# Two layer-1 blocks to a PSUM bank and one relu, quad-wise copies of the folded W_in, and a new early order, in a fused attention and squared-relu MLP

## The chip, the core and the metric

The kernel runs on one core of one Trainium2 chip. Its time is the device time of one execution in microseconds, the median of three runs. A profiled execution is a run of its own, with a time of its own and a span from the first to the last instruction. The engines, each with an instruction stream of its own that it works through in order: TensorE (PE, matmul), VectorE (DVE), ScalarE (ACT), GpSimd (POOL) and SyncE (SP). POOL issues all loads but that of the first p, and SP the stores.

## The reference

For each of 8 batches and 8 heads there are 576 rows of q, k and v (64 wide) and 32 rows of p. A first attention packs k and v into 32 rows; a second one lets q attend to these; the result, 4608 tokens of 512 numbers, goes through a two-layer MLP with a squared relu.

```python
p_packed = softmax(p @ k.T / 8) @ v              # 32 x 64 a head
x        = softmax(q @ p_packed.T / 8) @ p_packed  # 576 x 64 a head
h = x @ w_in            # x: [4608, 512], w_in: [512, 2048]
r = maximum(h, 0)
out = (r * r) @ w_out   # [4608, 512], float32
```

## The kernel before

**Names.** The order of all work is written out by hand: `ORDER` (L48) is a string of words, and `run` (L815) emits the instructions of one word after another, so that each engine gets its own in the order of the words. A word is a step, its numbers, and behind a colon the engine (`v` DVE, `a` ACT, `p` POOL). The heads of a batch are worked in two groups of four, called quads below: `m101` is the step `m1` of batch 0, quad 1.

**First attention of a batch.** `Lk`, `Lv`: loads (L291, L305). `kT`: DVE transposes k (L354). `s1`: scores on PE (L414). `m1`, `x1`: max (DVE, L437) and exponential (ACT, L451). `eT`, `eo`: PE transposes the exponentials, and a copy brings them out of PSUM (L461, L477). `pv`, `rd`, `pp`: times v, reciprocal, scaling (L488, L485, L519). `pt`, `po`: transpose of the packed rows and copy (L538, L546). `bd`, `bs` make a second form of them (L522, L530).

**Folding.** The packed rows are multiplied into W_in: `w`N (L616) makes the quarter N (512 of the 2048 columns) of a batch's own `wp` in two PSUM banks, one for each quad, and `W`N (L626) copies it out, both quads in one instruction of 1024 columns, or, with a third digit, one quad of 512 columns. `W201` is quarter 2 of batch 0, quad 1. W_in itself is loaded in six pieces `Wi` (L257): columns 0 to 511 and 512 to 1023 by 256 KB a quad, the last 1024 by 512 KB a quad. Quarters 2 and 3 need the last two pieces.

**Second attention.** `Lq` or `LA`, `LB`: loads of q (L275). Batches 0 and 1 are cut into a part A of 256 rows and a part B of 320 (`CUTS`, L40). For batch 0, PE transposes q (`QA`, `QB`, L371) and ACT copies it out (`EA`, `EB`); elsewhere DVE does it (`qA`, `qB`, `qT`). `z` or `s2`: scores on PE. `t`, `m`, `s`, `x`, `u`, `a`, `T` with A, B or 2: transpose, max, subtraction, exponential (ACT), sum with reciprocal, scaling, and the transpose that gives `a2T`, the operand of layer 1.

**The MLP.** `h`b.part.n (L650) makes block n (128 of the 2048 hidden columns) of a part: two matmuls (L638), one for each quad, of 256 or 320 columns in the first two batches, into a bank of its own. `r` (L656) is its relu, out of PSUM. `q` (L674) squares two blocks at once, SBUF to SBUF, into `gT`. `o`t.j (L685) is two matmuls of 512 columns for 128 tokens t; eight of them fill a bank, `c` copies it out and `d` stores it. Part A of batch 0 has tokens 0 to 255 (`o0`, `o1`). `H` and `R` (L662, L669) do two blocks with one relu; no word of `ORDER` uses them before.

**PSUM.** Eight banks: `psa` is two tiles of two banks each, for the attention's matmuls and `w`. Of the other four, three ("spare") and one ("idle") serve batch 0's attention and the fillers; from the first layer block on they are `x` and `y`, two banks each. The blocks of batch 0 take an `x` bank when n is even and a `y` bank when it is odd, those of later batches `y`; `o` takes `y` for t below 2 and `x` beyond. A bank is given out again when the last reader of the tile before it is done, and a step that needs one waits for that.

**Fillers.** `Z`n.m (L337) is n matmuls of 512 and m of 256 columns on zeros; nobody uses their result.

```python
    def busy(self, n, short):

        ps = self.banks("idle").tile([P, 512], F32, name="ps_idle")
        for m in [self.NE] * n + [self.NE // 2] * short:
```

The functions around the change:

Of the kernel before, what the change touches and what calls it, by code (L numbers as in the profile page):

```python
# [48 lines left out]
pf Lk00 P0 Lk01 kT00 Z14.0 s100 Lv00 LA0 kT01 m100 Z1.1 s101 m101 I x100 Lv01 x101 P1 Z2.1 eT00 LB0 eo00:v Z0.1 eT01  # L49
QA01 QA00 eo01:v Wi01 EA00:a rd0 pv0 pp0 EA01:a Z1.0 pt0 Wi00 po0:v Z0.1 zA0 tA00 Wi11 tA01 mA00 Z1.0 QB01 QB00 EB00:a  # L50
EB01:a mA01 sA00:v Wi10 Wi20 Z2.1 zB0 sA01:v xA00 xA01 tB00 Z5.0 w00 tB01 Wi21 mB00 W001:a Z3.0 w10 uA01 uA00 mB01
sB00:p aA01:p xB00 W000:a TA01 sB01:v aA00:p TA00 Lk11 uB00 W100:a h0.0.2 h0.0.3 Lk10 h0.0.0 xB01 h0.0.1 W101:a r0.0.3:a
h0.0.5 aB00:p uB01 Wo0 r0.0.2:a r0.0.0:v r0.0.1:a aB01:v h0.0.6 h0.0.7 h0.0.4 r0.0.5:a r0.0.6:a TB00 TB01 r0.0.4:v Lv10
r0.0.7:a h0.1.3 r0.1.3:a h0.1.6 q0.0.3:v h0.1.5 r0.1.6:v q0.0.0:v q0.0.2:v h0.1.2 h0.1.1 q0.0.1:a h0.1.0 r0.1.2:a w20
r0.1.5:a w30 r0.1.0:v h0.1.7 r0.1.1:a W30:a W20:v h0.1.4 Lv11 kT11 r0.1.4:a r0.1.7:a h0.0.9 h0.0.8 r0.0.9:a r0.0.8:a
h0.1.14 r0.1.14:a h0.1.15 q0.1.0:a q0.1.2:v kT10 Wo1 h0.0.13 r0.1.15:v h0.0.14 h0.0.12 q0.0.4:v q0.1.1:p s11 h0.0.11
r0.0.12:a h0.0.10 LB1 r0.0.13:a h0.1.13 r0.0.14:a m111 m110 r0.0.11:a h0.1.8 h0.0.15 r0.0.10:a x111 o2.0 x110 o2.1
r0.0.15:v r0.1.13:v eT11 h0.1.11 q0.0.5:v h0.1.9 q0.1.7:p r0.1.8:v eT10 r0.1.11:a rd1 h0.1.10 o0.0 r0.1.9:v eo11:a o1.0
LA1 eo10:v pv1 r0.1.10:v h0.1.12 pp1 q0.1.3:a o1.1 o0.1 bd1 r0.1.12:a pt1 q0.0.6:v o3.0 o3.1 q0.1.4:v po1:v w31 qB10 w11
q0.0.7:a o3.2 o1.2 qB11 W11:a o0.2 q0.1.6:v o0.3 W31:a qA10 o2.2 zB1 qA11 tB10 zA1 tA11 tB11 o3.3 tA10 Wo2 o2.3 mA10  # L60
mA11 o1.3 w21 mB10 mB11 q0.1.5:a Wo3 w01 sA11:v W21:a sA10:v xA11 sB11:v o2.4 uA11 o1.4 xA10 o1.5 uA10 o0.4 sB10:v o0.5
xB11 o0.6 o0.7 Pr o2.5 o1.6 aA10:v W01:a c0:a xB10 aA11:v Lk20 d0 TA10 TA11 o1.7 o3.4 Lv21 Lv20 uB11 c1:a o2.6 h1.0.1
Lk21 h1.0.6 Px o2.7 r1.0.1:v d1 r1.0.6:v o3.5 aB11:v h1.0.0 c2:a h1.0.2 Pt o3.6 r1.0.0:a TB11 o3.7 r1.0.2:a d2 Lk31 Pu
q1.0.0:a h1.0.4 h1.0.3 c3:a o4.0 r1.0.3:v r1.0.4:a o5.0 kT20 q1.0.1:a h1.0.7 d3 h1.0.5 uB10 o5.1 r1.0.5:a o4.1 r1.0.7:v
q1.0.2:a aB10:v h1.0.10 h1.0.8 q1.0.3:v r1.0.10:a o4.2 kT21 Lq2 h1.0.9 r1.0.8:a o5.2 r1.0.9:a h1.0.12 TB10 s12 q1.0.4:v
r1.0.12:a h1.0.14 m120 o5.3 Lv30 r1.0.14:a h1.1.1 m121 h1.1.3 r1.1.1:a o5.4 x120 r1.1.3:v h1.0.11 o4.3 r1.0.11:v x121
h1.1.7 kT31 h1.0.15 eT20 Lq3 q1.0.5:a o4.4 r1.0.15:v eT21 r1.1.7:v q1.0.7:a o5.5 rd2 eo20:v eo21:a h1.0.13 h1.1.2
r1.0.13:v o4.5 r1.1.2:v q1.0.6:a h1.1.6 pv2 r1.1.6:v h1.1.8 pp2 h1.1.0 q1.1.1:a r1.1.8:v Lk30 o5.6 qT21 q1.1.3:a o4.6
h1.1.12 r1.1.0:a bd2 pt2 qT20 o4.7 bs2:a Lk40 h1.1.5 po2:v r1.1.12:a o5.7 q1.1.0:v c4:a h1.1.10 r1.1.5:v c5:a s22 d4
r1.1.10:v h1.1.4 o6.0 t221 r1.1.4:a h1.1.9 d5 o7.0 q1.1.2:a t220 h1.1.13 r1.1.9:a o6.1 qT30 r1.1.13:a Lq4 h1.1.11  # L70
q1.1.4:a m221 w22 w32 r1.1.11:a o6.2 m220 W32:a h1.1.14 h1.1.15 W22:v Lv31 o6.3 r1.1.14:a q1.1.6:a o7.1 o6.4 sb21:v
r1.1.15:a Lv40 o7.2 q1.1.5:a kT30 o7.3 q1.1.7:a o7.4 sb20:v Lk41 x221 o6.5 qT31 o7.5 x220 o6.6 su21 o6.7 o7.6 su20 c6:a
o7.7 w02 a221:v c7:a d6 w12 o8.0 W02:a a220:v o8.1 d7 o8.2 aT21 W12:a o8.3 aT20 o8.4 Lq5 h2.0.1 h2.0.0 r2.0.1:v o8.5
r2.0.0:a o8.6 q2.0.0:v h2.0.2 h2.0.3 r2.0.2:v o9.0 Lk50 o8.7 r2.0.3:v h2.0.5 c8:a s13 q2.0.1:v r2.0.5:a h2.0.4 d8 m130
o10.0 r2.0.4:a h2.0.6 kT40 h2.0.7 r2.0.6:a o10.1 r2.0.7:a q2.0.2:v h2.0.10 Lk51 x130 m131 o9.1 h2.0.8 r2.0.10:a q2.0.3:v
o9.2 r2.0.8:a kT41 h2.0.13 x131 eT30 h2.0.9 r2.0.13:v o10.2 eo30:a rd3 r2.0.9:v h2.1.1 eT31 q2.0.4:v h2.0.14 r2.1.1:a
o10.3 r2.0.14:v eo31:a h2.0.11 Lk61 o9.3 r2.0.11:v o9.4 h2.0.12 h2.1.5 q2.0.5:v r2.0.12:a pv3 r2.1.5:v h2.0.15 q2.0.6:v
h2.1.4 pp3 r2.0.15:a o9.5 r2.1.4:v h2.1.6 bd3 pt3 q2.0.7:v h2.1.0 bs3:a o9.6 r2.1.6:v r2.1.0:v Lv41 po3:a o9.7 q2.1.2:v
# [56 lines left out]
class Kernel:  # L135
# [526 lines left out]
    def step_hh(self, engine, b, hf, fp):  # L662

        s0, s1 = self.part(b, hf)
        ps = self.ph[b, hf, fp, 2] = self.turn32("ps_hh")[:, :, :s1 - s0]
        for i in range(2):
            self.layer1(ps[:, i], b, 2 * fp + i, s0, s1)
# [202 lines left out]
```

## Time and profile before

| | |
|---|---|
| median of 3 runs | 240.57 us (240.53 to 240.69) |
| the profiled execution | 241.25 us |
| its span, first to last instruction | 239.4 us |
| busy: PE, DVE, ACT, POOL | 230.2, 200.2, 143.8, 72.4 us |
| first layer block of batch 0 (`h0.0.2`) starts | 20.65 us |
| first layer block of batch 1 (`h1.0.1`) starts | 47.56 us |
| loads: queue, share of 16 DMA engines | POOL's, 53.1% |
| moved from 15 to 20 us | 206 GB/s |

In a row of a timeline stand the start in us from the span's beginning, the length in us, the engine, the line of the kernel, the operation, what it writes and reads, the shape, and how many instructions follow each other in that row; behind it in brackets how long the engine was idle before, and what ended that. A wait that is put down to an engine that had long been done was ended by something else, often a DMA. The waits of an engine are listed as total, number and longest. Ends of matmuls are modelled, and a matmul is longer than the time to the next one's start.

### The profile page before, as it was taken

The page shows a single profiled execution, that of the slowest core. Times are in us where ns is not written, and L with a number is a line of the kernel's source. Part 1 is how long each engine was busy: PE and PEld are TensorE (multiplying, and loading weights), DVE is VectorE, ACT ScalarE, POOL GpSimd, SP SyncE. Part 2 cuts the span into 40 slices and gives each one's busy share as a digit, 9 for nine tenths or more (in the row PEclk, how much of TensorE's full clock was granted, in tenths as well). Part 3 has the DMA queues.
Part 4 walks back from the last instruction along what each step waited for, and adds up shares of the span by engine and source line. Part 5 has one row for each costly group of instructions (what it writes and reads, how often), then busy time and mean ns, then how long its engine had stood idle before and what let it go on. Part 6 is the DMA issues. An engine that isn't in the chain of part 4 may idle for free.

```text
span 239.4 us, 5971 instructions
## 1 busy us (share of the span) xinstructions
PE 230.2 (96%) x2355; PEld 123.7 (52%) x2355; DVE 200.2 (84%) x455; ACT 143.8 (60%) x311; POOL 72.4 (30%) x122
## 2 busy tenths in 40 slices
PE   8876999999999999999999999999999999999994
PEld 2533563456544564456555554565545644555543
DVE  2768986998997889989998889997899789987740
ACT  2347974887797657865693648774485346733300
POOL 8509573786676334054303340002000000000000
PEclk9999999999999999999999999999999999999999
DMA  6999999999999978469923993216112212111224
GB/s 103 195 205 214 204 211 204 152 246 190 198 208 183 239 98 120 69 85 202 123 68 36 201 131 55 52 43 96 44 24 67 49 44 45 45 45 45 49 60 111
DMA packets 30331, 28.50 MB, mean 119 GB/s; under 512 B 8160, under 2 KB 24288, under 8 KB 30304
## 3 DMA queue, kind: packets, MB, share of 16 engines
q0 software_dynamic: 23776, 18.55, 53.1%
q1 hardware_dynamic: 6384, 9.51, 14.9%
q8 instruction: 18, 0.29, 0.5%
q10 hardware_dynamic: 144, 0.07, 0.1%
q14 instruction: 9, 0.07, 0.1%
HBM read 37.22 MB, written 9.44 MB: 195 GB/s over the span
## 4 chain that ended last, share of the span: by engine, by line
PE 88%; DMA 5%; POOL 2%; DVE 1%; issue 1%; ACT 1%; ACTq 0%; POOLq 0%
PE ps_o L695 52%; PE ps_h L638 26%; DMA w_in_bf<-in_moe_w_in_dram 5%; PE ps_wp L623 3%; PE ps_s L411 3%; PE ps_e1T L474 2%; PE ps_pv L507 1%; POOL w_in_bf L259 1%; POOL q_b L271 1%; DVE r L645 1%; POOL k_b L271 1%; DVE wp L459 0%; ACT wp L457 0%; PE ps_pv L500 0%; PE ps_o L700 0%
## 5 line engine op out<-in xcount | busy, mean ns | idle before, releaser
L695 PE MATMUL ps_o<-w_out_bf,gT 128*128 128x512 bf16 (+1 forms) x576 | 147.0, 378 | 0.0
L638 PE MATMUL ps_h<-a2T,wp 128*128 128x288 bf16 (+2 forms) x512 | 89.7, 286 | 1.4 <-ACT r L643 0.9
L643 ACT ACTIVATE r<-ps_h 128x288 bf16<-128x288 f32 (+2 forms) x161 | 61.4, 413 | 48.5 <-PE ps_h L638 42.5
L695 PEld LDWEIGHTS <-gT 128*128 128x128 bf16 x576 | 54.5, 98 | 43.8 <-issue 3.3
L638 PEld LDWEIGHTS <-wp 128*128 128x128 bf16 x512 | 47.4, 98 | 42.5 <-issue 8.0
L645 DVE TENSOR_SCALAR r<-ps_h 128x288 bf16<-128x288 f32 (+2 forms) x95 | 41.3, 449 | 11.7 <-PE ps_h L638 10.5
L683 DVE TENSOR_TENSOR gT<-r 128x576 bf16<-128x576 bf16 (+2 forms) x108 | 46.5, 444 | 2.3 <-ACT r L643 1.4
L457 ACT CAST wp<-ps_wp 128x1024 bf16<-128x1024 f32 (+1 forms) x31 | 29.2, 962 | 9.5 <-PE ps_wp L623 9.5
L457 ACT COPY o_sb<-ps_o 128x512 f32<-128x512 f32 x26 | 15.2, 589 | 12.1 <-PE ps_o L695 11.7
L271 POOL DMA_DIRECT2D k_b<-in_k_dram x28 | 15.4, 554 | 14.4 <-DVE kT L357 6.8
L319 POOL DMA_DIRECT2D v_b<-in_v_dram x12 | 9.4, 782 | 34.1 <-PE ps_pv L507 28.5
L271 POOL DMA_DIRECT2D q_b<-in_q_dram x16 | 11.0, 690 | 25.3 <-DVE qT L369 23.4
L451 ACT ACTIVATE e<-ps_s,nm 128x576 bf16<-128x576 f32 x16 | 11.8, 742 | 7.0 <-DVE nm L437 6.8
L357 DVE STREAM_TRANSPOSE kT<-k_b 128x576 uint32<-128x576 uint32 x16 | 12.3, 771 | 3.0 <-DMA k_b<-in_k_dram 3.0
L591 DVE TENSOR_REDUCE sums<-e 128x18 f32<-128x576 f32 (+2 forms) x20 | 12.1, 606 | 0.6 <-ACT e L585 0.6
L681 ACT ACTIVATE gT<-r 128x640 bf16<-128x640 bf16 (+1 forms) x18 | 12.2, 694 | 0.4 <-DVE r L645 0.2
L437 DVE TENSOR_REDUCE nm<-ps_s 128x1 f32<-128x576 f32 x16 | 11.5, 739 | 1.0 <-PE ps_s L411 0.8
L341 PE MATMUL ps_idle<-gT 128*128 128x512 bf16 (+1 forms) x34 | 11.1, 458 | 1.2 <-DVE gT L190 1.2
L585 ACT ACTIVATE e<-d 128x576 f32<-128x576 f32 (+2 forms) x20 | 11.7, 600 | 0.8 <-DVE d L579 0.8
L369 DVE STREAM_TRANSPOSE qT<-q_b 128x576 uint32<-128x576 uint32 (+2 forms) x16 | 10.8, 683 | 1.1 <-DMA q_b<-in_q_dram 1.1
L579 DVE TENSOR_TENSOR d<-s,mx 128x576 f32<-128x576 f32 (+2 forms) x19 | 11.7, 641 | 0.0
L573 DVE TENSOR_REDUCE mx<-s 128x18 f32<-128x576 f32 (+2 forms) x20 | 11.6, 609 | 0.0
(68 smaller groups left out, 174.6 us busy)
## 6 DMA issues: line engine op xcount, KB each, us to landing
out_dram<-o_sb SPq DMA_DIRECT2D x65, 128.0 KB, 2.4
v_b<-in_v_dram POOLq DMA_DIRECT2D x12, 256.0 KB, 5.6
w_out_bf<-in_moe_w_out_dram POOLq DMA_DIRECT2D x4, 512.0 KB, 10.7
q_b<-in_q_dram POOLq DMA_DIRECT2D x6, 288.0 KB, 6.1
q_b<-in_q_dram POOLq DMA_DIRECT2D x12, 144.0 KB, 6.9
k_b<-in_k_dram POOLq DMA_DIRECT2D x12, 108.0 KB, 4.7
gT<-in_v_dram POOLq DMA_DIRECT2D x4, 288.0 KB, 8.5
w_in_bf<-in_moe_w_in_dram POOLq DMA_DIRECT2D x4, 256.0 KB, 11.7
```

What stands on the lines that cost most here:

```text
L271: engine.dma_start(x[n:], s[:P - n])
L357: self.nc.vector.transpose(t["kT"][:].rearrange("p s e -> p (s e)").bitcast(U32), t["k"][:].rearrange("p t d -> p (t d)").bitcast(U32))
L451: self.nc.scalar.activation(out, x, ACT.Exp, bias=t["nm"], accum_out=self.den[b][:, qd:qd + 1])
L457: engine.copy(out, x)
L579: engine.tensor_tensor(out=d2[:, x], in0=t["s2"][:, x], in1=t["mx"][:, x].unsqueeze(2).to_broadcast([P, n, NP]), op=ALU.subtract)
L591: nc.vector.reduce_sum(out=sums[:, x], in_=t["e2"][:, x], axis=AX.X)
L638: self.nc.tensor.matmul(ps, lhsT=self.att[b, 0]["wp"][:, qd, fb * P:(fb + 1) * P], rhs=self.att[b, qd]["a2T"][:, s0:s1], start=(qd == 0), ...
L643: engine.activation(r, ps, ACT.Relu)
L645: engine.tensor_scalar_max(r, ps, 0.0)
L681: engine.activation(out, r, ACT.Square)
L683: engine.tensor_tensor(out=out, in0=r, in1=r, op=ALU.mult)
L695: self.nc.tensor.matmul(self.o[tt][:, e], lhsT=self.gT[:, fb, a:a + P], rhs=self.w_out_bf[:, fb, e], start=(i == 0), stop=(i == self.NFB - 1))
```

## The change

- The sixteen blocks of batch 0's part A are made by eight `H` and taken out by eight `R`, all on ACT. `step_hh` takes one bank of `x` (odd pair) or `y` (even pair) for batch 0, with two blocks of 256 columns side by side, instead of a tile of `psa`. Before, sixteen `h` and sixteen `r`, thirteen of these on ACT and three on DVE.
- Quarters 2 and 3 of batch 0's `wp` are copied by quads, `W201` and `W301` on DVE, `W200` and `W300` on ACT. Before, `W20` on DVE and `W30` on ACT, 1024 columns each.
- The words ahead of `h2.0.1` stand in another order. Some go to another engine: `eo00`, `po1`, `W22` to ACT, `bs2`, `eo21` to DVE, and a number of relus and squares of batches 0 and 1 either way. `Lk11` and `Lk10` stand ahead of `sB00:p` on POOL, `Wi00` ahead of `Wi01`, `Lq2` ahead of `Lk21` and of batch 2's v's, `Lk31` behind `Lv31`; SP's stores go 2, 3, 1, 0, 4, 6, 5, 7. `QB00` stands ahead of `QB01`. `kT31` is the last DVE word ahead of batch 2's first relu.
- Fillers: three of 512 columns fewer and one of 256 more, and `w00` stands ahead of most of them.

From `h2.0.1` on both orders have the same words.

```diff
@@ -46,43 +46,42 @@ (ORDER; behind h2.0.1 the words are the same)
-pf Lk00 P0 Lk01 kT00 Z14.0 s100 Lv00 LA0 kT01 m100 Z1.1 s101 m101 I x100 Lv01 x101 P1 Z2.1 eT00 LB0 eo00:v Z0.1 eT01
-QA01 QA00 eo01:v Wi01 EA00:a rd0 pv0 pp0 EA01:a Z1.0 pt0 Wi00 po0:v Z0.1 zA0 tA00 Wi11 tA01 mA00 Z1.0 QB01 QB00 EB00:a
-EB01:a mA01 sA00:v Wi10 Wi20 Z2.1 zB0 sA01:v xA00 xA01 tB00 Z5.0 w00 tB01 Wi21 mB00 W001:a Z3.0 w10 uA01 uA00 mB01
-sB00:p aA01:p xB00 W000:a TA01 sB01:v aA00:p TA00 Lk11 uB00 W100:a h0.0.2 h0.0.3 Lk10 h0.0.0 xB01 h0.0.1 W101:a r0.0.3:a
-h0.0.5 aB00:p uB01 Wo0 r0.0.2:a r0.0.0:v r0.0.1:a aB01:v h0.0.6 h0.0.7 h0.0.4 r0.0.5:a r0.0.6:a TB00 TB01 r0.0.4:v Lv10
-r0.0.7:a h0.1.3 r0.1.3:a h0.1.6 q0.0.3:v h0.1.5 r0.1.6:v q0.0.0:v q0.0.2:v h0.1.2 h0.1.1 q0.0.1:a h0.1.0 r0.1.2:a w20
-r0.1.5:a w30 r0.1.0:v h0.1.7 r0.1.1:a W30:a W20:v h0.1.4 Lv11 kT11 r0.1.4:a r0.1.7:a h0.0.9 h0.0.8 r0.0.9:a r0.0.8:a
-h0.1.14 r0.1.14:a h0.1.15 q0.1.0:a q0.1.2:v kT10 Wo1 h0.0.13 r0.1.15:v h0.0.14 h0.0.12 q0.0.4:v q0.1.1:p s11 h0.0.11
-r0.0.12:a h0.0.10 LB1 r0.0.13:a h0.1.13 r0.0.14:a m111 m110 r0.0.11:a h0.1.8 h0.0.15 r0.0.10:a x111 o2.0 x110 o2.1
-r0.0.15:v r0.1.13:v eT11 h0.1.11 q0.0.5:v h0.1.9 q0.1.7:p r0.1.8:v eT10 r0.1.11:a rd1 h0.1.10 o0.0 r0.1.9:v eo11:a o1.0
-LA1 eo10:v pv1 r0.1.10:v h0.1.12 pp1 q0.1.3:a o1.1 o0.1 bd1 r0.1.12:a pt1 q0.0.6:v o3.0 o3.1 q0.1.4:v po1:v w31 qB10 w11
-q0.0.7:a o3.2 o1.2 qB11 W11:a o0.2 q0.1.6:v o0.3 W31:a qA10 o2.2 zB1 qA11 tB10 zA1 tA11 tB11 o3.3 tA10 Wo2 o2.3 mA10
-mA11 o1.3 w21 mB10 mB11 q0.1.5:a Wo3 w01 sA11:v W21:a sA10:v xA11 sB11:v o2.4 uA11 o1.4 xA10 o1.5 uA10 o0.4 sB10:v o0.5
-xB11 o0.6 o0.7 Pr o2.5 o1.6 aA10:v W01:a c0:a xB10 aA11:v Lk20 d0 TA10 TA11 o1.7 o3.4 Lv21 Lv20 uB11 c1:a o2.6 h1.0.1
-Lk21 h1.0.6 Px o2.7 r1.0.1:v d1 r1.0.6:v o3.5 aB11:v h1.0.0 c2:a h1.0.2 Pt o3.6 r1.0.0:a TB11 o3.7 r1.0.2:a d2 Lk31 Pu
-q1.0.0:a h1.0.4 h1.0.3 c3:a o4.0 r1.0.3:v r1.0.4:a o5.0 kT20 q1.0.1:a h1.0.7 d3 h1.0.5 uB10 o5.1 r1.0.5:a o4.1 r1.0.7:v
-q1.0.2:a aB10:v h1.0.10 h1.0.8 q1.0.3:v r1.0.10:a o4.2 kT21 Lq2 h1.0.9 r1.0.8:a o5.2 r1.0.9:a h1.0.12 TB10 s12 q1.0.4:v
-r1.0.12:a h1.0.14 m120 o5.3 Lv30 r1.0.14:a h1.1.1 m121 h1.1.3 r1.1.1:a o5.4 x120 r1.1.3:v h1.0.11 o4.3 r1.0.11:v x121
-h1.1.7 kT31 h1.0.15 eT20 Lq3 q1.0.5:a o4.4 r1.0.15:v eT21 r1.1.7:v q1.0.7:a o5.5 rd2 eo20:v eo21:a h1.0.13 h1.1.2
-r1.0.13:v o4.5 r1.1.2:v q1.0.6:a h1.1.6 pv2 r1.1.6:v h1.1.8 pp2 h1.1.0 q1.1.1:a r1.1.8:v Lk30 o5.6 qT21 q1.1.3:a o4.6
-h1.1.12 r1.1.0:a bd2 pt2 qT20 o4.7 bs2:a Lk40 h1.1.5 po2:v r1.1.12:a o5.7 q1.1.0:v c4:a h1.1.10 r1.1.5:v c5:a s22 d4
-r1.1.10:v h1.1.4 o6.0 t221 r1.1.4:a h1.1.9 d5 o7.0 q1.1.2:a t220 h1.1.13 r1.1.9:a o6.1 qT30 r1.1.13:a Lq4 h1.1.11
-q1.1.4:a m221 w22 w32 r1.1.11:a o6.2 m220 W32:a h1.1.14 h1.1.15 W22:v Lv31 o6.3 r1.1.14:a q1.1.6:a o7.1 o6.4 sb21:v
-r1.1.15:a Lv40 o7.2 q1.1.5:a kT30 o7.3 q1.1.7:a o7.4 sb20:v Lk41 x221 o6.5 qT31 o7.5 x220 o6.6 su21 o6.7 o7.6 su20 c6:a
-o7.7 w02 a221:v c7:a d6 w12 o8.0 W02:a a220:v o8.1 d7 o8.2 aT21 W12:a o8.3 aT20 o8.4 Lq5 h2.0.1 h2.0.0 r2.0.1:v o8.5
+pf Lk00 P0 Lk01 kT00 Z14.0 s100 Lv00 LA0 kT01 m100 Z0.1 s101 m101 I x100 Lv01 x101 P1 Z2.1 eT00 Z0.1 eT01 eo00:a QA00
+LB0 Wi00 eo01:v Wi01 QA01 pv0 Wi11 rd0 pp0 Wi10 EA00:a Z1.0 pt0 Wi20 EA01:a Wi21 po0:v Z0.1 zA0 Z1.0 QB00 tA01 tA00
+EB00:a mA01 Lk11 QB01 mA00 EB01:a sA01:v sA00:v xA00 Z1.1 zB0 xA01 tB00 tB01 mB00 w00 mB01 Lk10 uA00 uA01 sB01:v sB00:p
+W000:a aA00:p TA00 xB00 W001:a aA01:p Z7.1 w10 uB00 xB01 W101:a W100:a TA01 H0.0.1 aB00:p H0.0.2 uB01 Wo0 H0.0.0 H0.0.3
+R0.0.1:a R0.0.2:a R0.0.0:a aB01:v TB00 TB01 q0.0.0:v h0.1.1 h0.1.6 q0.0.1:v R0.0.3:a h0.1.5 q0.0.2:v r0.1.6:a h0.1.0
+h0.1.2 r0.1.1:a h0.1.7 r0.1.0:a q0.0.3:v Lv11 r0.1.5:v r0.1.2:a w20 h0.1.3 q0.1.0:v Lv10 w30 W201:v r0.1.7:a W200:a
+h0.1.4 r0.1.3:a W301:v H0.0.4 W300:a kT11 kT10 r0.1.4:a R0.0.4:a H0.0.7 q0.1.2:a h0.1.15 Wo1 h0.1.14 q0.0.4:v H0.0.6
+R0.0.7:a r0.1.15:a s11 H0.0.5 R0.0.6:a q0.1.1:p r0.1.14:v h0.1.11 R0.0.5:a h0.1.13 LB1 o2.0 m111 x111 h0.1.8 q0.1.7:p
+m110 r0.1.13:v x110 LA1 Wo2 o2.1 h0.1.9 r0.1.8:v eT11 h0.1.10 q0.0.6:v eT10 r0.1.9:v r0.1.11:a o1.0 eo11:a r0.1.10:v
+o1.1 h0.1.12 eo10:v q0.1.3:v rd1 pv1 pp1 o0.0 r0.1.12:a bd1 qB11 Wo3 o3.0 pt1 q0.0.7:v o0.1 o2.2 o1.2 po1:a q0.1.6:a
+qB10 qA10 w31 w11 o2.3 qA11 W31:a o3.1 W11:a o3.2 o3.3 zB1 zA1 q0.0.5:a tB11 tA10 tA11 Pr tB10 q0.1.4:a Lk20 o0.2 mA10
+mA11 o0.3 mB10 o1.3 w01 sA10:v w21 o1.4 o0.4 Lq2 sA11:v sB10:v W01:a o0.5 o2.4 o1.5 o1.6 o1.7 xA10 q0.1.5:a o0.6 o0.7
+xA11 uA10 o2.5 Lk21 o3.4 o3.5 aA10:v W21:a uA11 xB10 mB11 sB11:v aA11:v TA10 c1:a Lv21 TA11 c0:a uB10 xB11 h1.0.1 h1.0.0
+o2.6 r1.0.1:a o2.7 h1.0.2 r1.0.0:a uB11 Px h1.0.6 o3.6 o3.7 r1.0.2:v h1.0.3 c2:a r1.0.6:a q1.0.0:v h1.0.4 c3:a aB10:v
+r1.0.3:a r1.0.4:a kT20 o4.0 o5.0 TB10 h1.0.5 r1.0.5:a q1.0.1:v h1.0.12 Pt r1.0.12:v o5.1 o4.1 h1.0.9 Lv20 q1.0.2:a
+h1.0.7 r1.0.9:a o5.2 o4.2 aB11:v h1.0.10 Pu Lk30 TB11 Lq3 r1.0.7:a q1.0.3:a r1.0.10:a h1.0.8 kT21 r1.0.8:a s12 h1.1.1
+q1.0.4:a r1.1.1:a h1.0.14 m120 r1.0.14:v m121 o4.3 x120 o5.3 h1.1.7 r1.1.7:v h1.0.11 o4.4 qT21 eT20 r1.0.11:a h1.1.3
+h1.0.13 x121 Lv30 r1.1.3:v q1.0.5:v eo20:v o5.4 eT21 h1.1.0 eo21:v r1.0.13:a q1.0.6:a r1.1.0:a d2 qT20 h1.0.15 o4.5 d3
+r1.0.15:a o4.6 q1.1.0:a h1.1.12 r1.1.12:a h1.1.8 kT30 pv2 q1.0.7:a rd2 r1.1.8:v d1 h1.1.9 o5.5 pp2 bd2 r1.1.9:a h1.1.5
+o4.7 h1.1.2 r1.1.5:a bs2:v pt2 r1.1.2:a po2:v o5.6 c4:a s22 h1.1.13 q1.1.1:a h1.1.4 o5.7 o7.0 t220 r1.1.4:a q1.1.4:a
+r1.1.13:v h1.1.15 m220 h1.1.11 o7.1 w22 t221 w32 r1.1.15:a r1.1.11:a c5:a qT31 h1.1.10 d0 h1.1.6 o6.0 m221 r1.1.10:a
+q1.1.2:a o6.1 Lk40 r1.1.6:a h1.1.14 sb21:v o6.2 o7.2 q1.1.3:v W22:a o6.3 o7.3 r1.1.14:a o7.4 Lq4 o6.4 q1.1.5:v sb20:v
+Lv31 o7.5 x221 q1.1.6:a q1.1.7:v su21 x220 o6.5 o6.6 a221:v Lk31 o7.6 o6.7 qT30 w12 W32:a w02 su20 a220:v d4 o7.7 c6:a
+aT20 o8.0 d6 W02:a aT21 c7:a Lk41 d5 W12:a d7 o8.1 Lv40 o8.2 o8.3 Lq5 o8.4 kT31 h2.0.1 h2.0.0 r2.0.1:v o8.5 r2.0.0:a
...
@@ -662,7 +661,11 @@
     def step_hh(self, engine, b, hf, fp):
 
         s0, s1 = self.part(b, hf)
-        ps = self.ph[b, hf, fp, 2] = self.turn32("ps_hh")[:, :, :s1 - s0]
+        if b:
+            ps = self.turn32("ps_hh")
+        else:
+            ps = self.bank("x" if fp % 2 else "y", "ps_hh").rearrange("p (i s) -> p i s", i=2)
+        ps = self.ph[b, hf, fp, 2] = ps[:, :, :s1 - s0]
         for i in range(2):
             self.layer1(ps[:, i], b, 2 * fp + i, s0, s1)
 ```

## The prediction

> **What bounds the kernel now.** I read the page's engine table first, then the waits of TensorE (PE), then the timelines of the first 50 us engine by engine.
>
> ```profile
> span 239.4 us, 5971 instructions
> ...
> PE 230.2 (96%) x2355; PEld 123.7 (52%) x2355; DVE 200.2 (84%) x455; ACT 143.8 (60%) x311; POOL 72.4 (30%) x122
> ```
>
> The program is a stream of matmuls with next to no hole in it. All of PE's waits for the other engines' copies and for DMA sit at the start:
>
> ```profile
> PE ps_wp L623 <- DMA w_in_bf<-in_moe_w_in_dram: 1.3, 1, 1.3
> ...
> PE ps_h L638 <- ACT r L643: 0.9, 1, 0.9
> PE ps_h L638 <- DVE wp L459: 0.6, 1, 0.6
> ```
>
> The change removes no real matmul, so it can gain only what PE waits from the first layer block on, and lose only by new waits. The stretch in question, PE's timeline (start, length):
>
> ```profile
> 1.19 5.82 PE L341 MATMUL ps_idle<-gT 128*128 128x512 bf16 x14 [1.19 <-DVE gT L190]
> ...
> 16.43 0.26 PE L397 MATMUL ps_s<-qT,ppT 64*32 64x160 bf16 x8 [0.33 <-ACT qT L457]
> ...
> 17.86 0.41 PE L623 MATMUL ps_wp<-w_in_bf,ppT 64*32 64x512 bf16 x8
> ...
> 20.31 0.41 PE L623 MATMUL ps_wp<-w_in_bf,ppT 64*32 64x512 bf16 x8 [1.29 <-DMA w_in_bf<-in_moe_w_in_dram]
> 20.65 1.05 PE L638 MATMUL ps_h<-a2T,wp 128*128 128x256 bf16 x8
> 22.56 2.83 PE L638 MATMUL ps_h<-a2T,wp 128*128 128x256 bf16 x20 [0.86 <-ACT r L643]
> ...
> 27.17 1.85 PE L638 MATMUL ps_h<-a2T,wp 128*128 128x256 bf16 x14 [0.58 <-DVE wp L459]
> 28.95 0.71 PE L411 MATMUL ps_s<-kT,pT 32*32 32x192 bf16 x48
> ...
> 39.77 0.70 PE L411 MATMUL ps_s<-qT,ppd 32*32 32x320 bf16 x32
> ...
> 42.37 5.35 PE L695 MATMUL ps_o<-w_out_bf,gT 128*128 128x512 bf16 x24
> 47.56 0.60 PE L638 MATMUL ps_h<-a2T,wp 128*128 128x256 bf16 x4
> ```
>
> Prices from it: a 512-column matmul holds PE for (47.56-42.37)/24 = 0.216 us, a step `o` (two) 0.43; a 256-column layer matmul 0.108, so a block 0.22; a 320-column one 0.135, a block 0.27.
>
> **Fixed points.** Four moments in this stretch are set by DMA, which moves 206 to 213 GB/s from 15 us on whatever the order:
>
> ```profile
> 15.00:20.00 5.00, 3.45 (x37) 1.14 (x33) 4.50 (x15) 3.40 (x7) 1.86 (x4) 1.00 1.18 206
> 20.00:25.00 5.00, 3.83 (x35) 2.64 (x36) 4.28 (x14) 4.06 (x12) 4.76 (x9) 1.00 1.13 213
> ```
>
> Four views of loads: one narrowed to W_in's second piece (issue and time to landing, 11.4), one to its last piece (14.1), the DMA issues of 5 to 25 us (the 288 KB of k for kT10, 7.0), and POOL's timeline, which has the issue times of the last two:
>
> ```profile
> L259 POOL DMA_DIRECT2D w_in_bf<-in_moe_w_in_dram x1: 637/637/637, 6.4 to 6.4; - x1
> ...
> DMA to landing us min/median/max: 11.4/11.4/11.4
> ```
> ```profile
> DMA to landing us min/median/max: 14.1/14.1/14.1
> ```
> ```profile
> k_b<-in_k_dram POOLq DMA_DIRECT2D x1, 288.0 KB, 7.0
> ```
> ```profile
> 11.07 0.61 POOL L259 DMA_DIRECT2D w_in_bf<-in_moe_w_in_dram  x1 [0.66 <-DMA q_b<-in_q_dram]
> 18.14 0.72 POOL L579 TENSOR_TENSOR d<-s,mx 128x320 f32<-128x320 f32 x1 [6.45 <-DVE mx L573]
> ...
> 21.02 0.56 POOL L271 DMA_DIRECT2D k_b<-in_k_dram  x1
> ```
>
> So `w00` can't start before 6.4+11.4 = 17.8, `w10` not before 20.3 (its wait says so), `w20` not before 11.07+14.1 = 25.2, and kT10 not before 21.02+7.0 = 28.0. The other two engines of the stretch:
>
> ```profile
> 20.79 0.58 ACT L457 CAST wp<-ps_wp 128x512 bf16<-128x512 f32 x1 [0.96 <-PE ps_wp L623]
> 21.27 0.47 ACT L585 ACTIVATE e<-d 128x320 f32<-128x320 f32 x1
> ...
> 22.11 1.80 ACT L643 ACTIVATE r<-ps_h 128x256 bf16<-128x256 f32 x6
> ...
> 24.91 1.08 ACT L643 ACTIVATE r<-ps_h 128x320 bf16<-128x320 f32 x3
> 26.01 1.01 ACT L457 CAST wp<-ps_wp 128x1024 bf16<-128x1024 f32 x1
> ...
> 33.06 0.79 ACT L457 COPY e1T<-ps_e1T 96x768 bf16<-96x768 bf16 x1
> ```
> ```profile
> 19.47 0.31 DVE L613 STREAM_TRANSPOSE a2T<-a 128x128 uint32<-128x128 uint32 x1
> ...
> 20.28 0.30 DVE L613 STREAM_TRANSPOSE a2T<-a 128x128 uint32<-128x128 uint32 x1
> ...
> 21.78 0.49 DVE L591 TENSOR_REDUCE sums<-e 128x10 f32<-128x320 f32 x1 [0.59 <-ACT e L585]
> ...
> 23.12 0.56 DVE L613 STREAM_TRANSPOSE a2T<-a 128x160 uint32<-128x160 uint32 x2
> ...
> 25.90 1.21 DVE L459 CAST wp<-ps_wp 128x1024 bf16<-128x1024 f32 x1
> ...
> 28.10 0.77 DVE L357 STREAM_TRANSPOSE kT<-k_b 128x576 uint32<-128x576 uint32 x1
> ...
> 38.80 0.77 DVE L369 STREAM_TRANSPOSE qT<-q_b 128x256 uint32<-128x256 uint32 x2
> 40.33 1.58 DVE L568 STREAM_TRANSPOSE s<-ps_s 128x320 f32<-128x320 f32 x4 [0.75 <-PE ps_s L411]
> ...
> 46.57 0.50 DVE L613 STREAM_TRANSPOSE a2T<-a 128x128 uint32<-128x128 uint32 x2
> ```
>
> **The change, step by step.**
>
> *Up to `w10`.* `eo00` goes from DVE to ACT (0.79 by the row at 33.06); ACT is free there and DVE takes only `eo01`, so nothing moves. `EB00` comes after five transposes of ten, and `zB0` waited for it (0.33 at 16.43): an estimate of 0.3 gained, `zB0` ends at 16.4 instead of 16.7, and DVE's `tB00` begins so much earlier. `w00` still starts at 17.9: the fillers around it only change places, and PE now idles 1.5 us where it ran fillers. `Z7.1` (7x0.216+0.11, from 18.2) ends by 20.1, ahead of 20.3. Gain: 0.
>
> *POOL's queue.* The wait at 11.07 shows eight loads in flight: the 12th waits for the 4th. Lk11 and Lk10 now stand ahead of `sB00:p`. Their last issue waits for the 7th load, the first of W_in, which lands one 256 KB piece (1.3 us) ahead of 17.8, at 16.5, and is over by 17.1. `sB00:p` needs the max of `tB00`, near 17.8. Behind the wait stand `sB00`, `aA00`, `aA01`, `aB00` and Wo0; ACT's `xB00` and DVE's `TA` and `TB` wait for them. No cost; were that landing at 17.8, issue and all, `sB00` and its chain would come 0.6 late. DMA is full either way, so the k's land when they did.
>
> *The first blocks.* `TA01` was at 19.47, `TA00` at 20.28. DVE does the same work ahead of `TA00` but `TA01` (0.3), and begins 0.3 earlier: `TA00` at 19.7; then a sum with its reciprocal (0.49 and some 0.2), `TA01` 20.5 to 20.8. `H0.0.1` starts at 20.65 and waits 0.1 for `TA01`. `H0.0.2` needs both quads of `w10`, copied 20.79 and 21.27 (0.58 each): 21.9. So PE waits 0.6 there instead of 1.0 (21.5 to 22.56). Four H's are in four banks and wait for no relu. The other three H's take 1.3, and `h0.1` begins at 23.2 (was 23.5: eight blocks' matmuls of 0.108 from 22.56). Its `TB` were at 23.12, since `uB01` waited 0.59 for `xB01`, then behind W101 on ACT; now `xB01` is ahead of it, and `TB` end near 22.3.
>
> *The relus.* 16 relus of 256 become 8 of 512. Before shows none of 512: from above it is two of 256, 2x0.28 a start; from below, the slope of 256 to 320 (0.28 to 0.32) gives 0.44. I take the 512 cast, next start 0.48 after (20.79 to 21.27), length 0.58. ACT does all eight, so the handful of `h0.1` blocks ahead of `w20` waits 0.05 to 0.1 each; `w20` is DMA's at 25.2 anyway.
>
> *W_in's second half.* W20 and W30 took 1.21 and 1.01, side by side, and PE waited. By quads: `w20` ends at 25.65 (0.41 from 25.25); W200 on ACT 25.7 to 26.3, W201 on DVE half of 1.21, 0.6, to 26.35, and `H0.0.4` starts at 26.4. On ACT follow `r0.1.3` (26.2) and W300 (26.5 to 27.1), so `H0.0.7` starts at 27.15, having waited 0.35. Price of the split: one instruction more on each engine, beside PE. At 27.1 PE has done two blocks more (0.43) than at 27.17 before.
>
> *`s11`.* kT10 is DMA's (28.10+0.77): `s11` starts at 28.9 in both. PE now gets there at 28.55 and waits 0.35, one block (0.22) ahead of before, and 0.04 earlier. Ahead: 0.25. This is safe: all that comes before may be 0.35 worse and nothing changes.
>
> *To `zB1`.* From 28.95 to 39.77 are 10.82 us. Work in it: `s11` 0.64, three blocks of 256 (0.65), six of 320 (1.62), thirteen `o` (5.63), transposes, `pv1`, `w31`, `w11` 1.79: 10.33. So 0.49 is waiting, some 0.09 of it at each of three changes of matmul shape, which stay; 0.22 is waits for a bank. In the new order I find none (nearest: `H0.0.5` follows `s11`, 29.55 to 30.15, its relu ends at 30.8, and `h0.1.8`, which needs the bank, starts at 28.9+0.64+0.43+0.54+0.43 = 30.95). +0.22, and none of it if the new order has its own. `zA1` needs the transpose from 38.80 (to 39.6); PE gets there at 39.6: -0.02.
>
> *To `h1.0.1`.* Both orders have 28 `o` ahead of it, 15 behind `zA1`: 39.95 + 15x0.433 + 0.56 (two `w`) + 0.09 = 47.1, against 47.56. `TA11` ended at 47.07; its chain began at 40.33 and begins at 39.55 now, when `zB1` is out: 46.3, in time. Ahead 0.45.
>
> *47 to 77 us.* Same blocks, other sequence and engines (`bs2` to DVE, `W22` to ACT, kT31 behind `aT21`, d2 and d3 ahead of d1 and d0 on SP, Lq2 ahead of Lk21 and the v's on POOL). In the same way, before waits some 0.3 in all there. Bound: from +0.3 (all gone) down to a loss of one relu, 0.4, at each of two or three places. I take half gone: +0.15. Lq2 (576 KB) takes the place in the queue that the two v's (640 KB) had ahead of Lk21, so that k lands no later; kT21 then ends at 54.1, when PE wants `s12`. From `h2.0.1` on both orders are alike, and the lead is carried to the end.
>
> Sum: 0.25+0.22-0.02+0.15 = 0.6 us. The profiled execution took 241.25, 0.68 above the median of the three runs (240.57); 0.6 off both gives 240.65 and 240.0. 0.2% (0.48 us) is about what a measurement of this kernel tells from no change.
>
> The Trainium skill (ScalarE: Activation LUTs, What ACT_TABLE_LOAD costs) gives an ACTIVATE with immediate scale 186 ns + 0.833 N, overlapping the next by 93: 613 ns and a next start at 0.52 for 512, an estimate. For 256 columns it gives 399 ns, and six in 1.80 us agree. By it the last H relu would be 0.3 later and the sum 0.5.
>
> **Rivals.**
> *Hidden anyway.* The new order gets stuck as often as the old after `s11`: only 0 to 0.45 is left. For it: DMA, not relus, sets `s11` and `zA1`; against: the extra block. 240.1 to 240.6, about 240.35.
> *ACT becomes the bound (slower).* By the starts above ACT has next to no idle time from 20.8 to 30.8 in the new order. Each 0.01 in a 512 relu's next start delays R0.0.5 by 0.08, and with it `h0.1.8`, `x111`, `eT11` and batch 1's softmax. 0.2 is spare; at 0.58 a start the gain is gone, from 0.64 on it is slower. At 0.65: -1.4+0.2 against +0.6, 241.2. For it: all eight are on ACT; against: 0.56 is two of the old ones.
> *The clock falls.* PE idles 16.4 to 17.9. The fillers at 1.19 ran at 5.82/14 = 0.42, half speed, for 5.8 us. If that came again from 20.3, the 4.4 us of work there would take 4.4 more, less the 0.35: up to 244. Against: 1.29 us idle before 20.31, granted clock 1.00. The Trainium skill (TensorE: Matmul & The Clock Gate, Part 1) names an idle window of about 3.4 us; by that 1.5 does nothing.
> *A moved load is late (slower).* kT31 stands ahead of batch 2's first relu; Lk31 landing 1 us after `aT21` would hold `r2.0.1` and two banks, some 1.0: 241.0.
> *More.* All waits of 47 to 77 gone and `h0.1` smoother: 1.0, 239.6.
>
> **Chances.** Forecast (gain 0.48 to 0.8; 239.75 to 240.1) 0.42; more 0.07; hidden 0.31; ACT 0.11; clock 0.03; late load 0.06. Faster 0.49, same 0.31, slower 0.20. The range 239.5 to 241.1 leaves out the clock, half of ACT's case and the far end of "more".
>
> **What would show it.** Right: `w10` at 20.3; H0.0.2 at 21.9; no wait of 0.86 for a relu; `s11` at 28.9 again, behind kT10; `h1.0.1` near 47.1, `h2.0.1` near 76.2; 512 relus near 0.58. Wrong: `s11` later than 29.0; new rows among PE's waits after 30; kT31 behind a DMA; clock under 1.00 after 17.

## The result and the profile after

The change makes the kernel slower: 241.66 us (median of 14 runs, 240.95 to 242.84) against 240.68 (14 runs, 240.38 to 242.26), a ratio of 1.0039 with a 95% interval of 1.002 to 1.0058. The profiled execution took 241.65, its span is 239.9. Forecast was 240.0. (A ratio is the one on record, with its interval; it can differ by 0.1 or 0.2% from the quotient of the medians.)

PE's waits for other engines, after (us in total, times, longest):

```profile
PE ps_wp L622 <- DVE d L578: 1.0, 1, 1.0
PE ps_hh L637 <- ACT wp L456: 0.8, 3, 0.4
...
PE ps_hh L637 <- DVE a2T L612: 0.3, 1, 0.3
```

The wait of 0.9 for a relu is gone. In the place of the 0.6 for DVE's `W20` stand 0.8 for ACT's copies of `wp` (0.17 of it for `w10`'s). Where that is in time, PE's timeline after shows (start, length; answers to the rows shown of before):

```profile
20.23 0.41 PE L622 MATMUL ps_wp<-w_in_bf,ppT 64*32 64x512 bf16 x8 [1.04 <-DVE d L578]
...
21.84 1.48 PE L637 MATMUL ps_hh<-a2T,wp 128*128 128x256 bf16 x12 [0.17 <-ACT wp L456]
23.16 2.04 PE L637 MATMUL ps_h<-a2T,wp 128*128 128x320 bf16 x12
25.13 0.45 PE L622 MATMUL ps_wp<-w_in_bf,ppT 64*32 64x512 bf16 x8
...
27.10 0.61 PE L637 MATMUL ps_hh<-a2T,wp 128*128 128x256 bf16 x4 [0.43 <-ACT wp L456]
27.92 0.61 PE L637 MATMUL ps_hh<-a2T,wp 128*128 128x256 bf16 x4 [0.21 <-ACT wp L456]
...
29.44 0.71 PE L410 MATMUL ps_s<-kT,pT 32*32 32x192 bf16 x48
...
40.28 0.70 PE L410 MATMUL ps_s<-qT,ppd 32*32 32x320 bf16 x32
...
48.06 0.60 PE L637 MATMUL ps_h<-a2T,wp 128*128 128x256 bf16 x4
```

Up to `w20` (25.13) PE's moments named in the forecast stand within 0.15 us of it, but for `w00`, which came at 16.5 instead of 17.9 (its piece of W_in landed 0.8 sooner) and for which nothing waits. DVE's `TA01` ended 0.33 late, at 21.13; that is lost in the wait for `w10`'s copies. From there the first block that needs `w20`, `H0.0.4`, starts at 27.10 (forecast 26.4), `H0.0.7` at 27.92 (27.15), and `s11` at 29.44 (28.9). ACT's and DVE's timelines say why:

```profile
24.58 1.15 ACT L642 ACTIVATE r<-ps_h 128x320 bf16<-128x320 f32 x3
26.46 0.58 ACT L456 CAST wp<-ps_wp 128x512 bf16<-128x512 f32 x1 [0.74 <-DVE wp L458]
26.95 0.44 ACT L642 ACTIVATE r<-ps_h 128x320 bf16<-128x320 f32 x1
27.27 0.59 ACT L456 CAST wp<-ps_wp 128x512 bf16<-128x512 f32 x1
```
```profile
25.75 1.31 DVE L458 CAST wp<-ps_wp 128x512 bf16<-128x512 f32 x2
26.98 0.77 DVE L356 STREAM_TRANSPOSE kT<-k_b 128x576 uint32<-128x576 uint32 x1
27.90 0.78 DVE L356 STREAM_TRANSPOSE kT<-k_b 128x576 uint32<-128x576 uint32 x1 [0.15 <-DMA k_b<-in_k_dram]
```

`W200` did not run beside `W201`. ACT was free at 25.73 and stood for 0.74 us until DVE had ended its copy (0.68 long, from 25.75). `W300` came late behind it and behind the relu `r0.1.3`; it had no wait of its own here, since `W301` had ended at 27.06. `W200`'s wait is in the program: ACT's copy carries a wait for DVE's semaphore, which the copies of a whole tile on one engine do not have.

`w20` itself is set by DMA and moves by some tenths from execution to execution (24.39 to 25.31 in most profiles below). So the kernels are compared by what lies behind `w20`, from PE's timelines (us; differences of starts before rounding, and in the last two columns of the span to a tenth, so these are good to 0.05):

| kernel | `w20` to `s11` | to `zB1` | to `h1.0.1` | to the end | `w20` to the end |
|---|---|---|---|---|---|
| before | 3.64 | 10.82 | 7.78 | 191.84 | 214.09 |
| forecast | 3.65 | 10.38 | 7.82 | 191.7 | 213.5 |
| after | 4.31 | 10.84 | 7.78 | 191.84 | 214.77 |
| e1 own banks | 3.62 | 10.47 | 7.85 | 191.91 | 213.86 |
| e2 one engine per tile | 3.92 | 10.83 | 7.78 | 191.89 | 214.42 |
| e3 whole copies | 4.09 | 10.54 | 8.14 | 191.84 | 214.61 |
| e4 quads in old order | 4.40 | 10.62 | 7.78 | 191.85 | 214.65 |
| e11 pairs in old order | 4.12 | 10.76 | 7.78 | 191.84 | 214.50 |
| e13 seventh buffer | 4.19 | 10.40 | 7.78 | 191.81 | 214.18 |
| e14 three mended | 3.62 | 10.44 | 7.78 | 191.93 | 213.78 |

(The forecast's 3.65 is 28.9-25.25, its 191.7 the 191.84 of before less the 0.15 it took for 47 to 77 us.) The change loses 0.6 to 0.7 us against before, 0.67 of it ahead of `s11`. By then it has done a block more (0.22 of work), and that is spent again in waits before `zB1`. Behind `zB1` both are alike.

The other part is in the clock. Of the 14 executions of the changed kernel, four have a mean granted clock of 0.991 to 0.993 and take 242.56 to 242.84; the other ten have a median of 241.51. Below, "low" is an execution with a mean clock under 0.995.

### The profile page after: what moved, and what is told of

Read it like the earlier page. It is cut to its first block, busy times and chain, and to the rows that moved or that the text cites. A ratio compares the mean times of both kernels' runs of the same rounds, so it can differ in the third digit from the quotient of the medians.

```text
span 239.9 us, 5923 instructions
## 1 busy us (share of the span) xinstructions
PE 227.0 (95%) x2318; PEld 123.8 (52%) x2353; DVE 197.0 (82%) x448; ACT 146.1 (61%) x312; POOL 72.5 (30%) x122
## 4 chain that ended last, share of the span: by engine, by line
PE 78%; DVE 11%; DMA 3%; issue 3%; ACT 2%; POOL 1%; DVEq 0%; ACTq 0%; POOLq 0%
PE ps_o L698 46%; PE ps_h L637 22%; DMA gT<-in_v_dram 3%; PE ps_wp L622 3%; PE ps_s L410 2%; DVE gT L686 2%; DVE mx L572 1%; DVE d L578 1%; PE ps_e1T L473 1%; PE ps_pv L506 1%; ACT wp L456 1%; DVE s L564 1%; DVE r L644 1%; DVE sums L590 1%; PE ps_hh L637 1%
## 5 line engine op out<-in xcount | busy, mean ns | idle before, releaser
L698 PE MATMUL ps_o<-w_out_bf,gT 128*128 128x512 bf16 (+1 forms) x544 | 140.0, 378 | 2.1 <-issue 0.6
L642 ACT ACTIVATE r<-ps_h 128x288 bf16<-128x288 f32 (+2 forms) x156 | 60.5, 415 | 48.9 <-PE ps_h L637 45.4
L637 PE MATMUL ps_h<-a2T,wp 128*128 128x288 bf16 (+2 forms) x480 | 85.7, 287 | 0.3
L637 PEld LDWEIGHTS <-wp 128*128 128x128 bf16 x512 | 47.2, 98 | 41.9 <-issue 7.5
L686 DVE TENSOR_TENSOR gT<-r 128x576 bf16<-128x576 bf16 (+2 forms) x111 | 47.7, 444 | 3.5 <-ACT r L642 2.6
L644 DVE TENSOR_SCALAR r<-ps_h 128x288 bf16<-128x288 f32 (+2 forms) x84 | 36.8, 451 | 10.7 <-PE ps_h L637 9.5
L456 ACT CAST wp<-ps_wp 128x1024 bf16<-128x1024 f32 (+1 forms) x33 | 30.4, 940 | 6.8 <-PE ps_wp L622 5.8
L456 ACT COPY o_sb<-ps_o 128x512 f32<-128x512 f32 x26 | 15.3, 588 | 11.8 <-PE ps_o L698 11.4
L356 DVE STREAM_TRANSPOSE kT<-k_b 128x576 uint32<-128x576 uint32 x16 | 12.2, 764 | 3.2 <-DMA k_b<-in_k_dram 3.2
L622 PE MATMUL ps_wp<-w_in_bf,ppT 64*32 64x512 bf16 x256 | 10.8, 382 | 1.2 <-DVE d L578 1.0
L578 DVE TENSOR_TENSOR d<-s,mx 128x576 f32<-128x576 f32 (+2 forms) x19 | 11.8, 646 | 0.1
L598 DVE TENSOR_TENSOR a<-e,rs 128x576 bf16<-128x576 f32 (+2 forms) x17 | 11.7, 699 | 0.1
```

The source lines that it names most:

```text
L356: self.nc.vector.transpose(t["kT"][:].rearrange("p s e -> p (s e)").bitcast(U32), t["k"][:].rearrange("p t d -> p (t d)").bitcast(U32))
L456: engine.copy(out, x)
L578: engine.tensor_tensor(out=d2[:, x], in0=t["s2"][:, x], in1=t["mx"][:, x].unsqueeze(2).to_broadcast([P, n, NP]), op=ALU.subtract)
L622: self.nc.tensor.matmul(ps[NP * g:NP * g + NP, qd, :], lhsT=self.att[b, qd]["ppT"][r, NP * h:NP * h + NP], rhs=self.w_in_bf[r, h, f:f + se ...
L637: self.nc.tensor.matmul(ps, lhsT=self.att[b, 0]["wp"][:, qd, fb * P:(fb + 1) * P], rhs=self.att[b, qd]["a2T"][:, s0:s1], start=(qd == 0), ...
L642: engine.activation(r, ps, ACT.Relu)
```

## The experiments

Three theories. **A**: the two engines' copies of one PSUM tile go by turns. **B**: ACT has too much to do with eight relus of 512. **C, D**: the loss lies elsewhere in the new order, or in the clock.

### The copies: e1 to e4

e1 gives each quad of `w20` and `w30` a PSUM tile of its own, and has one relu earlier so that a bank is free:

```diff
-        ps = self.att[b, 0]["ps_wp", n] = self.turn32("ps_wp")
+        if b == 0 and n in range(2, 4):
+            ps = [self.bank(x, "ps_wp") for x in "xy"] if n == 2 else [self.turn32("ps_wp")[:, 0, :] for _ in range(2)]
+        else:
+            ps = self.turn32("ps_wp")
...
-h0.1.5 q0.0.2:v r0.1.6:a
+h0.1.5 r0.1.5:v q0.0.2:v r0.1.6:a
...
-Lv11 r0.1.5:v r0.1.2:a w20
+Lv11 r0.1.2:a w20
```

> The change, but the two quads of w20 are written to two PSUM tiles of their own (one bank of pool x, one of y), and those of w30 to two tiles of the large pool; r0.1.5 goes ahead of q0.0.2 on DVE so that its bank is free for w20. Same matmuls, same copies on the same engines. Theory A (in the changed kernel ACT's copy W200 may not start before DVE's copy W201 of the same PSUM tile has ended, 26.46 instead of 25.75; likewise W300 behind W301): W200 starts by 25.8 beside W201, H0.0.4 at 26.4 to 26.6 (was 27.10), H0.0.7 at 27.2 (was 27.92), s11 at 28.75 to 28.9, behind kT10 (DVE ended it at 28.68); 0.5 to 0.7 us less than the change, so a ratio of 1.001 to 1.002 against before. Rival B (ACT has too much to do with the 512 relus, and the copies would be late anyway): H0.0.4 stays at 27.0 or later, s11 at 29.4, ratio 1.004. Rival C (what is lost lies behind s11 or in the clock): s11 moves but the time does not, ratio 1.004.

Measured: 240.51 (12 runs), ratio 0.9991 (0.9971 to 1.0011). ACT's, DVE's and PE's timelines of e1:

```profile
25.11 0.58 ACT L457 CAST wp<-ps_wp 128x512 bf16<-128x512 f32 x1
...
26.07 0.58 ACT L457 CAST wp<-ps_wp 128x512 bf16<-128x512 f32 x1
```
```profile
25.21 0.68 DVE L459 CAST wp<-ps_wp 128x512 bf16<-128x512 f32 x1
26.11 0.69 DVE L459 CAST wp<-ps_wp 128x512 bf16<-128x512 f32 x1 [0.21 <-PE ps_wp L627]
```
```profile
24.64 0.41 PE L627 MATMUL ps_wp<-w_in_bf,ppT 64*32 64x512 bf16 x8
...
26.22 1.13 PE L646 MATMUL ps_hh<-a2T,wp 128*128 128x256 bf16 x8
...
28.27 0.45 PE L411 MATMUL ps_s<-kT,pT 32*32 32x192 bf16 x24
```

The same copies on the same engines now run side by side, `H0.0.4` starts 1.58 us behind `w20` instead of 1.97, and `s11` 3.62 instead of 4.31. The interval of the ratio ends (1.0011) below where that of the change begins (1.002). ACT has the same relus as in the change, so B is not what made the copies late. The wait hangs on the tile, not on the bank: a `ps_wp` tile has 2x512 f32 a partition and each quad lies in its own half of 2 KB. The Trainium skill (PSUM — Partial Sum Buffer, Specifications and PSUM bank collisions) gives 2 KiB a partition as one bank and tells of a compiler's scheduler that adds a dependency between instructions on different engines that touch the same bank (in the same 32 partitions). Here a tile of two banks got one as well. What would happen without the wait no run here shows.

e2 and e3 take the sharing away in other ways, e4 puts the quads alone into the old order:

```diff
 e2
-w30 W201:v r0.1.7:a W200:a h0.1.4 r0.1.3:a W301:v H0.0.4 W300:a
+w30 W201:v r0.1.7:a W200:v h0.1.4 r0.1.3:a W301:a H0.0.4 W300:a
 e3
-w30 W201:v r0.1.7:a W200:a h0.1.4 r0.1.3:a W301:v H0.0.4 W300:a
+w30 W20:v r0.1.7:a W30:a h0.1.4 r0.1.3:a H0.0.4
 e4 (kernel before)
-r0.1.1:a W30:a W20:v h0.1.4
+r0.1.1:a W201:v W200:a W301:v W300:a h0.1.4
```

> The change with W200 on DVE and W301 on ACT, so that DVE copies all of w20's tile and ACT all of w30's: same four instructions, two on each engine. Theory A: no copy waits for another engine's; DVE 25.75 to 27.06, ACT about 26.35 to 27.4; H0.0.4 at 27.1 as in the change, H0.0.7 right behind it at 27.55 (was 27.92), s11 at 29.07 (was 29.44), 0.37 less than the change: ratio 1.002. Rival B: ACT has the same work, H0.0.7 stays at 27.9, s11 at 29.4, 1.004. Rival C: s11 moves, the time does not.

> The change with W_in's second half copied out as before: W20 whole on DVE, W30 whole on ACT (1024 wide, 1.21 and 1.01 us). Theory A: 25.75 to 26.97 on DVE, 26.35 to 27.35 on ACT, H0.0.4 at 27.0, H0.0.7 at 27.45, s11 at 28.97: 0.4 to 0.5 less than the change, ratio 1.002. Rival B: s11 at 29.4 or later, 1.004. Rival C: s11 moves, the time does not.

> The kernel before with one edit: W30 and W20 replaced by the change's four quads (W201 on DVE, W200 on ACT, W301 on DVE, W300 on ACT). Theory A: the copies go by turns here too (W200 on ACT 26.5 to 27.1, W301 beside it, W300 27.2 to 27.8); h0.0.9 starts at 27.17 as before, and the blocks that need w30 come three blocks later, at 28.2, so that s11 stays at 28.95: ratio 0.999 to 1.001. Rival B and C: the copies are not at fault, ratio 1.000 and W200 beside W201.

Measured: e2 241.22, ratio 1.0023 (0.9999 to 1.0047); e3 241.49, 1.0023 (0.9999 to 1.0047); e4 241.27, 1.0007 (0.9988 to 1.0026). e2's `s11` comes 3.92 behind `w20`, which is the expected 0.37 less than in the change. e3 gives back 0.22 of the expected 0.4 to 0.5: `H0.0.6` then comes 0.17 later, behind a relu. e4 refutes its expectation: in the old order too the quads cost, `s11` comes 4.40 behind `w20` instead of 3.64. PE's timeline of e4:

```profile
26.59 0.61 PE L638 MATMUL ps_h<-a2T,wp 128*128 128x256 bf16 x4 [0.67 <-ACT wp L457]
27.52 1.59 PE L638 MATMUL ps_h<-a2T,wp 128*128 128x320 bf16 x10 [0.32 <-ACT r L643]
```

The relus stand behind the late copies on ACT, and PE waits for these next. So in the profiles the split of one tile over two engines costs some 0.7 us at `s11` in either order. The times of e2, e3 and e4 alone do not show it: their intervals take in 1 (e4's median is 0.54 above the 240.73 of before there).

### The clock: e5 to e10

The new order keeps the fillers in other places. Five edits put fillers back or take one out; e10 is the changed kernel once more:

```diff
 e5 (on e1)       -m100 Z0.1 s101       +m100 Z1.1 s101
 e6 (on e1)       -mB00 w00             +mB00 Z5.0 w00
 e7 (on e1)       both of these, and    -w10 uB00   +w10 Z2.0 uB00
 e8 (on before)   -m100 Z1.1 s101       +m100 Z0.1 s101
 e9 (the change)  -mB00 w00             +mB00 Z5.0 w00
```

> The kernel with own banks (e1) with one filler matmul of 512 put back ahead of s101 (Z1.1 for Z0.1, as in the kernel before). Of the executions of the kernels in the new order 15 of 52 had a mean granted clock of 0.991 to 0.993 and were 1.2 to 1.5 us longer; of those in the old order 1 of 47. Theory D1 (the gap of PE at 7.5 to 8.4 us, just after the warm-up, lets the clock fall): no execution of 12 under 0.995; median 240.4, ratio 0.998. Theory D2 (the idle time between 16 and 20 us does it): 3 or 4 of 12 under 0.995, ratio as e1, 0.999. Theory D3 (chance): no pattern over the four kernels.

> The kernel with own banks (e1) with five fillers put back ahead of w00 (Z5.0, 1.1 us, as in the kernel before); Z7.1 behind it stays. w00 ends at about 17.9 instead of 17.0, Z7.1 ends by 19.6, ahead of w10, so nothing on the way to w10 is late. D2: no execution under 0.995, ratio 0.998. D1: 3 or 4 of 12 under 0.995, ratio 0.999.

> The kernel with own banks with both fillers of e5 and e6, and two more (Z2.0, 0.43) between w10 and the first layer block, which waits 0.5 there for a2T anyway. D1 and D2: no execution under 0.995; median 240.3, spread under 1 us; ratio 0.998 (0.5 us less than before). If the two fillers delay the first block by 0.4 us, h1.0.1 stays where it is, since w20 is set by DMA.

> The kernel before with the one filler of 512 ahead of s101 taken out (Z0.1 for Z1.1, as in the changed kernel), nothing else. D1: 3 or 4 of 12 executions under 0.995, 1.2 us or more longer, median 0.1 to 0.3 up, ratio 1.001. D2: none of 12 under 0.995, ratio 1.000.

> The change as it is, with the five fillers of the kernel before put back ahead of w00 (as in e6), nothing else. If the shared tile and the clock are two causes that add up: no execution under a clock of 0.995, but W200 still starts when W201 has ended, s11 still 4.3 us behind w20, and the median at 241.3 to 241.5, ratio 1.002 to 1.003. If the filler were the whole cause: ratio 1.000.

> The changed kernel itself, on the chip of e9, e11 and e12. 3 or 4 of 12 executions under a clock of 0.995, those 1.2 us longer than the others; median 241.5, ratio 1.004. By theory A it stands 0.5 to 1.0 us above e12.

(The count in e5's expectation should be 16 of 50, not 15 of 52.)

| kernel | low, of executions | median of the others | ratio to before, all executions |
|---|---|---|---|
| after; e10 | 4 of 14; 4 of 12 | 241.51; 241.57 | 1.0039; 1.0031 (1.0008 to 1.0054) |
| e9 (after and fillers) | 0 of 12 | 241.62 | 1.0021 (0.9999 to 1.0043) |
| e1; e2; e3; e5 | 2; 4; 6; 3 of 12 | 240.47; 241.14; 240.94; 240.67 | e5: 1.0 (0.9977 to 1.0023) |
| e6 | 0 of 12 | 240.78 | 0.9996 (0.9982 to 1.001) |
| e7 | 0 of 12 | 240.62 | 0.9991 (0.9976 to 1.0005) |
| e8 (before and one less) | 0 of 12 | 240.62 | 0.9999 (0.9982 to 1.0015) |

With e11 to e15 below: in the new order without fillers ahead of `w00` 30 of 86 executions are low, with them none of 72; in the old order 5 of 180. So the filler at `s101` has no part in it (e5, e8: D1 falls), the five ahead of `w00` end it (D2). They do not mend the copies: e9 stays at 241.62, its `s11` 4.32 behind `w20`. In time e6 and e7 come out above the ratio of 0.998 that was expected of them. The profile of e13 (the change with one more buffer, below) is of a low execution; its row of the granted clock in 40 slices, the same by microseconds (PE busy first, the clock before the last two numbers), and PE's timeline:

```profile
PEclk9998899999999999999999999999999999999999
```
```profile
18.00:19.00 1.00, 0.51 (x3) 0.10 (x1) 0.96 (x4) 0.24 (x1) 0.72 (x1) 1.00 1.15 213
19.00:20.00 1.00, 0.15 (x8) 0.14 (x8) 0.97 (x4) 0.70 (x2) 0.97 (x2) 1.00 1.11 209
20.00:21.00 1.00, 0.53 (x9) 0.17 (x2) 0.97 (x5) 0.98 (x3) 0.49 (x2) 1.00 1.14 213
21.00:22.00 1.00, 0.95 (x8) 0.65 (x8) 0.93 (x3) 0.81 (x2) 1.00 (x2) 1.00 1.11 211
22.00:23.00 1.00, 1.00 (x9) 0.73 (x7) 0.61 (x3) 0.94 (x3) 1.00 (x3) 0.60 1.11 209
23.00:24.00 1.00, 1.00 (x6) 0.65 (x5) 0.57 (x2) 0.74 (x2) 1.00 (x2) 0.50 1.11 210
24.00:25.00 1.00, 1.00 (x5) 0.56 (x4) 0.87 (x3) 0.53 (x2) 0.14 (x1) 0.50 1.14 214
25.00:26.00 1.00, 1.00 (x7) 0.64 (x5) 0.49 (x1) 0.71 (x3) 0.00 (x0) 0.70 1.11 219
```
```profile
16.72 1.79 PE L340 MATMUL ps_idle<-gT 128*128 128x512 bf16 x8
19.85 0.41 PE L622 MATMUL ps_wp<-w_in_bf,ppT 64*32 64x512 bf16 x8 [1.34 <-DMA w_in_bf<-in_moe_w_in_dram]
...
21.05 2.57 PE L637 MATMUL ps_hh<-a2T,wp 128*128 128x256 bf16 x15 [0.52 <-DVE a2T L612]
23.41 2.88 PE L637 MATMUL ps_h<-a2T,wp 128*128 128x320 bf16 x12
26.22 0.41 PE L622 MATMUL ps_wp<-w_in_bf,ppT 64*32 64x512 bf16 x8
```

The clock is at half for about 3.4 us (0.40, 0.50, 0.50 and 0.30 lost in four microseconds, and half speed loses 0.50 in one), from 22.2 to 25.6, just where the first layer blocks run; `w20`, otherwise DMA's at about 25, becomes PE's at 26.22. That is 1.1 us, and the low executions after are 1.2 above the others. The Trainium skill (TensorE: Matmul & The Clock Gate, Part 1) has the gate judge by free-running windows of about 3.4 us, which fits the length and that only some executions are hit; that it takes an idle window does not fit, since PE's longest hole here is 1.34. In the profile of before the hole is as long (1.29) and PE is busy for less between 19 and 22.5 (1.41 us against 2.13 in e13), but the old order is hit in 5 of 180. What the gate counts stays open: e13's is the only profile of a low execution.

### The pairs alone: e11

```diff
 (kernel before, step_hh as in the change)
-h0.0.2 h0.0.3 Lk10 h0.0.0 xB01 h0.0.1 W101:a r0.0.3:a h0.0.5 aB00:p
+H0.0.1 Lk10 xB01 H0.0.0 W101:a R0.0.1:a H0.0.2 aB00:p uB01 Wo0 R0.0.0:a aB01:v H0.0.3 R0.0.2:a
...
-h0.0.13 r0.1.15:v h0.0.14 h0.0.12 q0.0.4:v q0.1.1:p s11 h0.0.11
+H0.0.6 r0.1.15:v H0.0.7 q0.0.4:v q0.1.1:p s11 R0.0.6:a H0.0.5
...
```

> The kernel before with the pairs alone: two blocks of batch 0's first piece in one PSUM bank and one relu of 512 on ACT (H and R for the sixteen h and r), W_in copied as before, the rest of the order kept; s11 then has 24 blocks ahead of it instead of 23. If the pairs are worth what the prediction took: the 512 relus 0.58 to 0.6 long and 0.48 from start to start, no wait of 0.86 for a relu, s11 3.6 to 3.9 us behind w20, ratio 0.998 to 1.000. Rival B (all eight on ACT are too much): blocks after s11 wait for R0.0.5 or R0.0.7, zB1 later than 10.8 us behind s11, ratio 1.001 or more.

Measured: 241.11, ratio 0.9997 (0.9976 to 1.0018). The relus' row (least, median, most in ns) and its answer after:

```profile
L639 ACT ACTIVATE r<-ps_hh x8: 592/598/618, 21.4 to 30.4; 128x512 bf16<-128x512 f32 x8
```
```profile
L642 ACT ACTIVATE r<-ps_hh x8: 592/601/662, 21.8 to 30.7; 128x512 bf16<-128x512 f32 x8
```

The relus are as long as forecast. In the old order the pairs gain nothing, and behind `w20` they lose 0.4: `s11` at 4.12, with one block more ahead of it (0.22), and since `H0.0.6` starts 0.31 late, behind a relu on ACT. So rival B is real there, though it did not decide the change.

### What was late behind s11: e13

After, 10.84 us lie between `s11` and `zB1`; 10.38 were forecast. DVE's timeline after has `r0.1.8` late:

```profile
31.56 0.48 DVE L644 TENSOR_SCALAR r<-ps_h 128x320 bf16<-128x320 f32 x1
32.45 0.49 DVE L644 TENSOR_SCALAR r<-ps_h 128x320 bf16<-128x320 f32 x1 [0.41 <-issue]
```

Its block's matmuls were done at 31.95. It carries a wait for POOL's semaphore, which was taken to be for the square `q0.1.7`, as the reader of the buffer that it is to write.

```diff
-        self.rp = pool("rp", 6)
-        self.op = pool("op", 5)
+        self.rp = pool("rp", 7)
+        self.op = pool("op", 4)
```

> The change with seven buffers for the relus' output instead of six (and four instead of five for the outputs' staging, to make room), nothing else. In the change r0.1.8 on DVE writes the buffer that POOL's q0.1.7 reads, and starts 3.01 us behind s11; in e1, e3, e5, e6 and e7 it starts 2.60 to 2.65 behind. Theory P (it waits for POOL's q0.1.7): it now starts at 2.6 to 2.65, PE's waits for h0.1.10 and the next o (0.18 and 0.25 in the change) go, zB1 10.5 behind s11 instead of 10.84, 0.3 us less than the change: median at full clock 241.2, ratio 1.0015 to 1.003. Theory I (an issue delay of DVE that no buffer explains): 3.01 and 10.84 as in the change, ratio as the change's, 1.003 to 1.004.

Measured: 241.75, ratio 1.0036 (1.0016 to 1.0056); 7 of 12 are low (so is the profile), and the other five have a median of 240.88. DVE's timeline, `s11` at 30.41:

```profile
32.53 0.98 DVE L644 TENSOR_SCALAR r<-ps_h 128x320 bf16<-128x320 f32 x2
```

The two relus are now back to back, `r0.1.8` 2.61 behind `s11`, and `zB1` 10.40 behind it: the signs of theory P. But POOL's timeline after, and DVE's before, speak against P:

```profile
30.22 1.25 POOL L686 TENSOR_TENSOR gT<-r 128x640 bf16<-128x640 bf16 x1 [0.78 <-ACT r L642]
```
```profile
31.48 0.82 DVE L645 TENSOR_SCALAR r<-ps_h 128x256 bf16<-128x256 f32 x2 [0.32 <-issue]
```

The square had ended at 31.47, 0.98 us before `r0.1.8` began, and "issue" stands for no releaser that the profile shows. In e1, e3, e5, e6 and e7 a relu with the same wait starts 2.60 to 2.65 behind `s11`, with the square at nearly the same place; and before has a late relu too. So e13's edit takes the late start away, but that the relu waited for POOL is not shown, and what held DVE stays open. (A lead that no run tests: in the six profiles with the late start, those of before, after, e2, e8, e9 and e10, the late relu is the 64th instruction recorded on DVE, waits for semaphores counted; in the profiles where a relu with the same two waits, PE's and POOL's, is the 63rd or 67th, it starts at most 0.16 late.)

### All together: e12, e14, e15

e12 (on e6) moved more words in order to save the 0.18 that `h0.1.3` waits for a relu; e14 is e6 with e13's buffers; e15 swaps two blocks in e14.

```diff
 e12
-Lv11 r0.1.2:a w20
+Lv11 r0.1.7:a w20
...
-W201:v r0.1.7:a W200:a
+W201:v r0.1.2:a W200:a
...
-H0.0.7 q0.1.2:a h0.1.15
+H0.0.7 h0.1.15
...
-r0.1.15:a s11 H0.0.5 R0.0.6:a
+r0.1.15:a q0.1.2:a H0.0.5 s11 R0.0.6:a
 e15
-w20 h0.1.3
+w20 h0.1.4
...
-W200:a h0.1.4 r0.1.3:a
+W200:a h0.1.3 r0.1.4:a
...
-kT10 r0.1.4:a
+kT10 r0.1.3:a
```

> e6 (own banks, filler ahead of w00) with three moves on ACT and PE: r0.1.7 ahead of r0.1.2 (in e6 h0.1.3 waited 0.27 for it), q0.1.2 behind r0.1.15, H0.0.5 ahead of s11. No copy waits for the other engine's, no execution under 0.995, and PE has 26 blocks behind it when s11 starts. s11 behind kT10 or right after H0.0.5, 3.9 to 4.0 us behind w20; h1.0.1 21.7 behind w20 (22.25 before, 22.93 in the change). Ratio 0.997 to 0.999. If s11's later place makes batch 1's softmax late, a new wait stands between s11 and zB1 and the ratio is 1.000.

> The change with all three causes taken away: own PSUM tiles for the four quads (e1), five fillers ahead of w00 (e6), seven relu buffers (e13). If these three are the whole miss: no execution under a clock of 0.995, s11 3.65 behind w20, zB1 10.4 to 10.5 behind s11, h1.0.1 21.9 behind w20 (the forecast's 21.85), and from there to the end as before, since the forecast's 0.15 us for 47 to 77 us was not there: 0.4 us less than before, ratio 0.998 to 0.999. If something else is still late: ratio 1.000 or more.

> e14 with h0.1.4 (and its relu) ahead of h0.1.3: in e6, h0.1.3 waited 0.27 behind w20 for the relu r0.1.7, whose bank it needs, while h0.1.4's bank is free. If PE is what counts from w20 on: that wait goes, s11 3.4 to 3.6 behind w20 (not sooner than kT10, which ended 3.5 behind w20 in e6), h1.0.1 21.65 to 21.8; ratio 0.997 to 0.998, better than both kernels. If kT10 sets s11: 3.6 and 21.9, as e14.

e12: 241.28, 1.0003 (0.9982 to 1.0024), a miss. `h0.1.3` waits as before, `s11` comes 4.18 behind `w20` for the block put ahead of it, and a relu on DVE is late behind it. e14: 240.36, ratio 0.9982 (0.9967 to 0.9996), none of 12 low. e15: 240.51, 0.998 (0.9967 to 0.9994): the wait at `h0.1.3` is gone, but PE then waits for kT10, and it is no better than e14. Both are some 0.2% under before, with intervals that end just under 1. PE's timeline of e14 at `w20`, `s11`, `zB1` and `h1.0.1`:

```profile
24.82 0.54 PE L627 MATMUL ps_wp<-w_in_bf,ppT 64*32 64x512 bf16 x8
...
28.45 0.71 PE L411 MATMUL ps_s<-kT,pT 32*32 32x192 bf16 x48
...
38.89 0.70 PE L411 MATMUL ps_s<-qT,ppd 32*32 32x320 bf16 x32
...
46.67 0.60 PE L646 MATMUL ps_h<-a2T,wp 128*128 128x256 bf16 x4
```

`h1.0.1` is 21.84 behind `w20`. The forecast had 21.85 (47.1 less 25.25), the change has 22.93, before 22.24. So with the three edits the whole miss up to there is gone. Most of it goes with the first: e1 alone, where no relu is late either, has 21.95. What the seventh buffer adds to e6 is not located.

## Why the prediction was wrong

- *Up to `w10`, the first blocks, the relus*: right. `w10` 20.23 (20.3), `H0.0.2` 21.84 (21.9), `h0.1` 23.16 (23.2), `w20` 25.13 (25.25), a relu of 512 0.60 long (0.58). The estimate of 613 ns that follows from the Trainium skill (ScalarE: Activation LUTs, What ACT_TABLE_LOAD costs) is a little nearer. The prediction found its figures for 256 columns to agree with six relus in 1.80 us; with the overlap of 93 they make 1.93.
- *W_in's second half*: this step failed. "W200 on ACT 25.7 to 26.3, W201 on DVE half of 1.21, 0.6, to 26.35" took for granted that two engines copy out of one PSUM tile at once, and put the price of the split at one instruction more. What the runs show in its place: ACT's copy waits 0.74 us for DVE's, and with a tile for each copy (e1) it does not. Before shows no such pair: its two copies ran side by side out of two tiles. The bound from the other side, one after the other, would have been 0.6, and what it costs is 0.66 at `s11` against the forecast. DVE's copy of 512 also takes 0.68, not half of 1.21.
- *`s11` at 28.9, "safe: all that comes before may be 0.35 worse"*: the copies made it 0.89 worse, 29.44 against PE's forecast arrival at 28.55. kT10 was there at 28.68. The block ahead (0.22) is real, but `s11` is 0.54 late.
- *To `zB1`, +0.22, "in the new order I find none"*: this failed too. Only PE's banks were looked through, not DVE's starts: `r0.1.8` starts 0.41 late, as a relu of before does by 0.32, and 10.84 instead of 10.38 follows. Without the late start (e13) it is 10.40, so the rest of the term was right; the cause of the late start is open.
- *47 to 77 us, +0.15*: nothing. From `h1.0.1` to the end both take 191.8, to 0.1.
- *The clock falls, 0.03*: the moment was named (from 20.3 on), the chance was ten times too small and the size (4.4 less 0.35) over three times too large. About a third of the executions are hit, for 1.2 us. "1.29 us idle before 20.31, granted clock 1.00" was one profiled execution, which cannot show what happens in some of them. The change's fillers "only change places" was costed at nothing; that place was the cover.
- *ACT becomes the bound*: not the cause (e1), but seen in e11.
- Of the sum, 0.6 gained, e14 has 0.44 (240.36 against 240.80 of before on that chip), with the three edits. Of the 1.66 between forecast and measured median, 0.66 is the copies, 0.46 the way to `zB1`, 0.15 the gain that was not there from 47 to 77 us, and 0.15 the low executions (241.66 against 241.51); the rest, some 0.2, is not located.

## What to carry to other kernels

When a copy is split over two engines, look at what the halves share, not only at who is free: a tile that two engines read got a wait between them here, and the split cost what it was to save; with two tiles there was no such wait. When a late step carries a wait for a slow engine, look when that engine had ended: here it was 0.98 us before the step began, and an edit that took the late start away did not show its cause. And a filler that only moves still has to be costed over many executions, since one profile cannot show a clock that falls in every third.

## What was not expected of the hardware

- The granted clock halved for about 3.4 us though PE had been busy for 1.63 of the 3 us before (0.15, 0.53 and 0.95) and its longest hole was 1.34 us (e13). By their mean granted clock it did so in 30 of 86 executions of the new order, and in none of 72 with five fillers of 0.22 us more.
- Half a copy is not half the time: DVE takes 0.68 us for 512 columns from PSUM and 1.21 for 1024, ACT 0.58 and 1.01.
- In six profiles, before and after among them, a DVE relu starts 0.3 to 0.4 us late with nothing in the profile to release it; a POOL square that it might have waited for had ended 0.98 us earlier (after).
